# Moving the sign of a converted weight chunk behind the next exponentials on ScalarE

## The chip, the cores and the metric

The kernel runs on one core of one Trainium2 chip. The metric is device time in microseconds (us) from start to end of one execution; lower is better. The engines named below are TensorE (PE in the profile: matmuls and transposes), VectorE (DVE), ScalarE (ACT), GpSimd (POOL) and SyncE (SP, which here only issues DMAs). Each engine works through its own instruction stream in order; semaphores hold an instruction back until what it needs is done on another engine. DMAs move data between DRAM and on-chip memory.

## The reference

An attention block is followed by a Fourier mixing block, all in float32. There are 8 batches, 8 heads, 576 positions and 64 dimensions per head.

```python
scores = scale * np.matmul(q, k.transpose(0, 1, 3, 2))
thresh = np.max(scores, axis=-1, keepdims=True) - tau
scores = np.where(scores >= thresh, scores, -1000000000.0)
scores = scores - np.max(scores, axis=-1, keepdims=True)
attn = np.exp(scores)
attn = attn / (np.sum(attn, axis=-1, keepdims=True) + 1e-09)
x = np.matmul(attn, v)            # then (B,H,S,D) -> (B, S, H*D)
X = np.fft.fft(np.fft.fft(x, axis=1), axis=2)
u = x + np.real(X)
un = (u - mean(u)) / np.sqrt(var(u) + 1e-06)
out = u + np.maximum(un @ w_ch1, 0.0) @ w_ch2
```

The two weight matrices, w_ch1 (512 x 2048) and w_ch2 (2048 x 512), come in as float64, since the set-up casts q, k and v to float32 but not these. [...]the kernel converts them itself, from the raw bits.

## The kernel before

**Attention in steps.** Heads are taken in pairs, four pairs to a batch. A pair is worked off in five steps of 128 queries: steps t = 0 to 3 have both heads, step t = 4 takes the last 64 queries of both heads in one tile. A step's number is i, and 20 steps make a batch. `scores(i)` puts the scores into two PSUM tiles on TensorE (L430, L436). `softmax(i)` then runs, per head: the negated row maximum on VectorE (L453, `neg`), the exponential on ScalarE (L461, `e`), the threshold on ScalarE (L465, `thr`, once for both heads), and on VectorE the masking with its row sum (L469, which needs `thr` and `e`). After it come the reciprocal of the sums (L481) and, in the first batches, a broadcast copy of it on GpSimd (L493, `rec`). `transposed_weights(i - 1)` turns the masked weights of the step before with TensorE transposes (L530, L533, L548), and ScalarE copies them out of PSUM (`ends`, L536 and L540; `e_t`, L550 and L552). `weighted_values` multiplies them with V on TensorE (L577) and takes the result over on VectorE (L585). In t = 3, `prep_pair` transposes the next pair's K and Q on VectorE (L401 to L404), once their loads have come.

**Conversion of the weights.** It is spread over the first two batches, 16 chunks of 128 x 512 for w_ch1 in the first (one per step, steps 0 to 15) and 16 for w_ch2 in the second (the table `PLAN` gives the step of each; in three steps there are two chunks). `convert` is a generator, and each `yield` ends a stage:

- a DMA brings the raw 64-bit words into a stage in memory (L287); four stages in the tile `hs` are used in turn, in the second batch also other tiles;
- VectorE masks the mantissa bits (L297) and the exponent bits (L300) out of the high words;
- ScalarE scales the mantissa (L305), makes the bits of a power of two from the exponent (L308, `power`), and takes the sign of the high word, into the high word's own place (L311, `sign`);
- VectorE adds the low words (L313);
- GpSimd multiplies by the power (L318) and by the sign (L319), both in place in the weight tile.

In the first batch, `step(i)` issues the VectorE stage of chunk i before the transposed weights, and its ScalarE stage behind them. So on ScalarE the order around a step boundary is: `ends`, `e_t`, L305, L308, L311 of chunk i, and then the exponentials of step i + 1. The two stages left run inside `softmax(i + 1)`, as `meanwhile`, that is between the maxima and the exponentials: L313 on VectorE and L318 with L319 on GpSimd. The load of chunk i + 3 is issued at the end of step i. The second batch does the same through `advance(first)` and `advance(first - 1)`, where `first` counts the steps of that batch; when two chunks share a step, `advance` takes one stage of each in turn. There the steps also hold parts of other work: the Fourier mixing and the first matmuls of the channel part (`hidden`, L810, with its ReLU taken alternately by ScalarE, L815, and VectorE, L817), and the rows of finished tokens with their means and variances (`Rows.load`, L770 to L779; `Rows.factors`, L784).

**What sets the order.** For the first two batches the order of every engine is that of the program text (a manual schedule); from the third batch on only TensorE's order is written out by hand. In the first batch TensorE also runs a few matmuls on constants (`busy`, L112) that fill its time.

Of the kernel before, what the change touches and what calls it, by code (L numbers as in the profile page):

```python
# [47 lines left out]
def kernel(  # L48
# [12 lines left out]
    nc = tc.nc  # L61
# [218 lines left out]
    def convert(src, dst, raw, power):  # L280

        if src.dtype == FP32:
            nc.sync.dma_start(out=dst, in_=src)
            return
        nc.sync.dma_start(out=raw, in_=src.bitcast(INT32).rearrange("p (c n) -> p c n", c=2))  # L287
        pairs = raw.rearrange("p c (n two) -> p c n two", two=2)
        low, high = pairs[:, :, :, 0], pairs[:, :, :, 1]
        dst = dst.rearrange("p (c n) -> p c n", c=2)  # L290
        bits = dst.bitcast(INT32)
        power = power.rearrange("p (c n) -> p c n", c=2)
        sign = high.bitcast(FP32)

        yield

        nc.vector.tensor_scalar(  # L297
            out=bits, in0=high, scalar1=0xFFFFF, scalar2=None, op0=ALU.bitwise_and
        )
        nc.vector.tensor_scalar(  # L300
            out=power, in0=high, scalar1=20, scalar2=0x7FF,
            op0=ALU.logical_shift_right, op1=ALU.bitwise_and,
        )
        yield
        nc.scalar.activation(out=dst, in_=bits, func=ACT.Copy, bias=1.0, scale=2.0**-20)  # L305


        nc.scalar.activation(  # L308
            out=power, in_=power, func=ACT.Relu, bias=shift[:, :], scale=float(1 << 23)
        )  # L310
        nc.scalar.activation(out=sign, in_=high, func=ACT.Sign)  # L311
        yield
        nc.vector.scalar_tensor_tensor(  # L313
            out=dst, in0=low.bitcast(UINT32), scalar=2.0**-52, in1=dst,
            op0=ALU.mult, op1=ALU.add,
        )
        yield
        nc.gpsimd.tensor_tensor(out=dst, in0=dst, in1=power.bitcast(FP32), op=ALU.mult)  # L318
        nc.gpsimd.tensor_tensor(out=dst, in0=dst, in1=sign, op=ALU.mult)  # L319

    def chunk(src, dst, raw, power):
# [117 lines left out]
                )  # L439
        steps[i] = (sc, nh)  # L440

    def softmax(i, between=None, meanwhile=None):

        t = i % NT
        sc, nh = steps[i]
        neg = sb.tile([128, 2], FP32, tag="neg", bufs=3, name="neg")
        thr = sb.tile([128, 2], FP32, tag="thr", bufs=3, name="thr")
        den = sb.tile([128, 2], FP32, tag="den", bufs=3, name="den")


        e = sb.tile([128, 2 * S], FP32, tag="e", name="e")
        for j in range(nh):
            nc.vector.tensor_reduce(  # L453
                out=neg[:, j : j + 1], in_=sc[j][:, :, 0:HALF], axis=AXIS_XY, op=ALU.max,
                negate=True,
            )
        if meanwhile is not None:
            meanwhile()
        for j in range(nh):
            ej = e[:, S * j : S * (j + 1)].rearrange("p (c n) -> p c n", c=2)  # L460
            nc.scalar.activation(  # L461
                out=ej, in_=sc[j][:, :, 0:HALF], func=ACT.Exp, bias=neg[:, j : j + 1], scale=1.0
            )
            if j == 0:
                nc.scalar.activation(  # L465
                    out=thr[:, 0:nh], in_=neg[:, 0:nh], func=ACT.Identity,
                    bias=thr_off[:, :], scale=-1.0,
                )
            nc.vector.scalar_tensor_tensor(  # L469
                out=ej, in0=sc[j][:, :, 0:HALF], scalar=thr[:, j : j + 1], in1=ej,  # L470
                op0=ALU.is_ge, op1=ALU.mult, accum_out=den[:, j : j + 1],
            )

            nc.vector.tensor_scalar(
                out=den[:, j : j + 1], in0=den[:, j : j + 1], scalar1=1e-9, scalar2=None,
                op0=ALU.add,
            )
            if between is not None:
                between()
                between = None  # L480
        nc.vector.reciprocal(den[:, 0:nh], den[:, 0:nh])  # L481
        rec = None
        if normalized(i // NT):
            nc.vector.tensor_scalar(
                out=e[:, 0:S], in0=e[:, 0:S], scalar1=den[:, 0:1], scalar2=None, op0=ALU.mult
            )
            if nh == 2:
                nc.scalar.activation(  # L488
                    out=e[:, S : 2 * S], in_=e[:, S : 2 * S], func=ACT.Copy, scale=den[:, 1:2]
                )  # L490
        else:
            rec = sb.tile([128, 2 * D], FP32, tag="rec", name="rec")
            nc.gpsimd.tensor_copy(  # L493
                rec[:, :].rearrange("p (j d) -> p j d", j=nh), _repeated(den[:, 0:nh], 2 * D // nh)
            )
        if t == 4:
            nc.scalar.copy(e[:, S : S + 64], e[:, 512:S])
        steps[i] = (e, rec)
# [674 lines left out]
    def step(i):  # L1173

        n, t = divmod(i, NT)
        scores(i)

        def last_stages():
            run = chunks.pop(i - 1, None)
            for _ in range(2 if run else 0):  # L1180
                next(run, None)

        if t == 1 and n > 0:
            softmax(i, lambda: weighted_values(n - 1, 1), last_stages)
            load_v(n + 1)
        elif t == 3:
            softmax(i, lambda: weighted_values(n, 0), last_stages)
        else:
            softmax(i, None, last_stages)
        if t == 1 and n > 0:  # L1190
            pass
        elif later and later[0][0] <= i:
            later.pop(0)[1](i)
        else:
            busy(2 if i < NCHUNK else 1)
        if t == 2:
            scale_q(n + 1)
        if t == 3:
            prep_pair(n + 1)
        if t == 1:  # L1200
            prep_ends(n)
        if i in chunks:
            next(chunks[i])
        if i > 0:
            transposed_weights(i - 1)
        if i in chunks:
            next(chunks[i])
        while after and after[0][0] <= i:
            after.pop(0)[1]()
        if i > 0 and i + 3 < NCHUNK:  # L1210
            chunks[i + 3] = w1_chunk(i + 3)
        if t == 2 and n > 0:
            folds.append(fold_rows(n - 1))
        if folds and next(folds[0], True):
            folds.pop(0)
# [56 lines left out]
    def advance(at):  # L1272
        for run in chunks.get(at, ()):
            next(run, None)
# [34 lines left out]
    def second_batch(i):  # L1309

        nonlocal budget
        n, t = divmod(i, NT)
        first = i - per_batch
        if first != 1:
            scores(i)
        if first == 0:

            transposed_weights(i - 1)
        softmax(i, None, lambda: (advance(first - 1), advance(first - 1)))
        chunks.pop(first - 1, None)  # L1320
        transfers(first)
        fold_more()
        if first == 0:
            weighted_values(n - 1, 1)
            scores(i + 1)
            column_means(LAST)
            copy_mean(LAST)
            folds.append(fold_rows(n - 1))
            while folds:
                fold_more()  # L1330
            load_v(n + 1)
            start_batch(0)
            mix(3)
            mix(3)
        elif first == 1:
            mix(3)
            transposed_weights(i - 1)
            mix(2)
            mirrored(LAST)
            for c, eng in ((1, nc.vector), (3, nc.vector), (0, nc.gpsimd), (2, nc.gpsimd)):  # L1340
                less_mean(eng, LAST, c)
            advance(first)
            advance(first)
        elif first == 2:
            mix(2)
            transposed_weights(i - 1)
            mix(2)
            weighted_values(n, 0)
            advance(first)
            advance(first)  # L1350
        else:
            fill()
            transposed_weights(i - 1)
            advance(first)
            advance(first)
            fill()
            if t == 3:
                prep_pair(n + 1)
            fill()
            if t == 2:  # L1360
                weighted_values(n, 0)
            if t == 0:
                weighted_values(n - 1, 1)
                folds.append(fold_rows(n - 1))
                load_v(n + 1)
        if t == 1:
            prep_ends(n)
        if t == 2:
            scale_q(n + 1)
        if first == 16:  # L1370
            fold_halves(1)
        if first < 3:
            budget += 3 * per_slot
# [95 lines left out]
```

## Time and profile before

| | value |
|---|---|
| time, median of 5 runs | 1635.12 us (1634.53 to 1636.62) |
| time of the profiled execution | 1635.14 us |
| its span, first to last instruction | 1633.2 us |
| TensorE busy | 1583.7 us (97%) |
| VectorE busy | 1171.9 us (72%) |
| ScalarE busy | 816.3 us (50%) |
| GpSimd busy | 659.4 us (40%) |
| mean granted TensorE clock | 0.995 |

An engine's busy time is an average over parts of the program with different limits. Engine names in the rows below are the profile's; PEld is TensorE's weight load, which overlaps its matmuls. A row of the groups gives line, engine, operation, tiles, shapes and count, then the busy time and the mean of one instruction, then the engine's idle time before them with the one that ended it. A row in order of time gives start, duration, engine, line and operation, and in brackets the idle time of that engine before it and who ended it. Neighbouring instructions of an engine overlap a little in the records, so what one costs in its queue is the distance from its start to the next one's start.

### The profile page before, as it was taken

To read this page: it belongs to the slowest core of one execution; us is meant where nothing else is said; L and a number is where in the kernel's file an instruction comes from. 1 tells how busy PE (TensorE), PEld (TensorE's weight loads), DVE (VectorE), ACT (ScalarE), POOL (GpSimd) and SP (SyncE) were. 2 spreads that over 40 slices of the span, in tenths; PEclk is the share of its full clock that TensorE was granted. 3 is DMA by queue.
4 is the path that set the end of the run, shared out by engine and by line. 5 is a ranking of instruction groups with operands and counts; after the bars stand their busy time and mean duration, and the time that the engine had idled before them with its cause. 6 is when DMAs were issued, how large, how long until landed. Compare 5 with 4: busy or idle time off the path is not lost.

```text
span 1633.2 us, 27899 instructions
## 1 busy us (share of the span) xinstructions
PE 1583.7 (97%) x10346; PEld 1247.0 (76%) x10346; DVE 1171.9 (72%) x2518; ACT 816.3 (50%) x1738; POOL 659.4 (40%) x875
## 2 busy tenths in 40 slices
PE   8998889999999999999999999999999999999998
PEld 4555555577887888878888778877878788889998
DVE  7887896667757687857676868786787869664445
ACT  5775675544555454545354546454646455523111
POOL 6784674042421553244342244224352344125332
PEclk9999999999999999999999999999999999999999
DMA  6423222101110101110011010111111110000000
GB/s 160 124 56 113 74 74 57 36 22 22 18 41 15 33 12 43 23 28 16 22 23 36 15 36 9 43 23 29 23 22 36 23 28 2 14 7 7 14 14 14
DMA packets 203085, 57.41 MB, mean 35 GB/s; under 512 B 193828, under 2 KB 193830, under 8 KB 202951
## 3 DMA queue, kind: packets, MB, share of 16 engines
q1 hardware_dynamic: 200438, 55.34, 14.5%
q8 instruction: 82, 1.34, 0.4%
q10 hardware_dynamic: 2512, 0.30, 0.1%
q14 instruction: 53, 0.43, 0.1%
HBM read 46.02 MB, written 9.44 MB: 34 GB/s over the span
## 4 chain that ended last, share of the span: by engine, by line
PE 76%; DVE 14%; ACT 5%; issue 2%; POOL 1%; DMA 1%; SPq 0%; DVEq 0%; POOLq 0%; ACTq 0%
PE ph L914 24%; PE po L1078 20%; PE pv L577 9%; PE sc L430 7%; PE pw L548 6%; PE po L836 3%; DVE e L469 3%; DVE neg L453 2%; ACT e L461 2%; PE sc L436 1%; PE ph L810 1%; PE py L680 1%; PE pa L697 1%; PE pn L770 1%; DVE hs L1039 1%
## 5 line engine op out<-in xcount | busy, mean ns | idle before, releaser
L453 DVE TENSOR_REDUCE neg<-sc 128x1 f32<-128x576 f32 x288 | 207.1, 747 | 163.1 <-PE sc L430 151.9
L461 ACT ACTIVATE e<-sc,neg 128x576 f32<-128x576 f32 x288 | 212.2, 737 | 216.0 <-DVE neg L453 215.7
L469 DVE SCALAR_TENSOR_TENSOR e<-sc,thr,e 128x576 f32<-128x576 f32 x288 | 229.4, 811 | 49.9 <-ACT thr L465 48.4
L1078 PE MATMUL po<-w,hs 128*128 128x256 f32 x1024 | 246.9, 384 | 0.0
L1078 PEld LDWEIGHTS po<-w,hs 128*128 128x128 f32 x1024 | 186.5, 190 | 34.1 <-issue 13.0
L914 PE MATMUL ph<-u_t,w 128*128 128x128 f32 x1536 | 187.0, 276 | 0.0
L430 PE MATMUL sc<-kT,qT 64*128 64x288 f32 x1024 | 173.0, 431 | 11.8 <-DVE e L469 10.6
L914 PEld LDWEIGHTS ph<-u_t,w 128*128 128x128 f32 x1536 | 179.0, 192 | 5.0 <-issue 3.7
L548 PE MATMUL pw<-ident,e 128*128 128x128 f32 x1152 | 170.1, 274 | 8.1 <-ACT y_o L685 2.3
L550 ACT COPY e_t<-pw 128x512 f32<-128x512 f32 x256 | 148.6, 593 | 48.9 <-PE pw L548 48.2
L923 DVE TENSOR_TENSOR hs<-ph,hs 128x512 f32<-128x512 f32 x160 | 106.8, 684 | 69.5 <-PE ph L914 53.8
L548 PEld LDWEIGHTS pw<-ident,e 128*128 128x128 f32 x1152 | 134.4, 141 | 27.6 <-issue 4.2
L430 PEld LDWEIGHTS sc<-kT,qT 64*128 64x128 f32 x1024 | 95.4, 186 | 76.5 <-issue 36.5
L914 PE MATMUL ph<-t_u,s_w 128*128 128x128 f32 x1024 | 126.4, 277 | 2.2 <-POOL t_u L888 1.8
L914 PEld LDWEIGHTS ph<-t_u,s_w 128*128 128x128 f32 x1024 | 119.5, 192 | 7.7 <-issue 4.9
L1078 PE MATMUL po<-hs,s_tile 128*128 128x256 f32 x512 | 121.5, 381 | 0.0
L792 DVE SCALAR_TENSOR_TENSOR u<-po,rstd,u 128x256 f32<-128x256 f32 (+1 forms) x164 | 75.2, 482 | 64.0 <-PE po L1078 62.9
L488 ACT ACTIVATE e<-e,den 128x576 f32<-128x576 f32 x96 | 74.5, 776 | 76.5 <-DVE den L481 76.0
L1078 PEld LDWEIGHTS po<-hs,s_tile 128*128 128x128 f32 x512 | 94.0, 190 | 13.7 <-issue 2.5
L931 ACT ACTIVATE hs<-hs 128x512 f32<-128x512 f32 x112 | 69.2, 629 | 62.0 <-DVE hs L923 62.0
L610 POOL TENSOR_TENSOR half<-x 128x287 f32<-128x287 f32 x48 | 40.2, 858 | 119.8 <-ACT x L583 61.1
L1074 POOL TENSOR_TENSOR hs<-hs,s_tile 128x512 f32<-128x512 f32 x32 | 42.1, 1316 | 109.5 <-PE po L1078 86.5
(194 smaller groups left out, 2898.5 us busy)
## 6 DMA issues: line engine op xcount, KB each, us to landing
hs<-in_moe_w_ch_dram SPq DMA_DIRECT2D x23, 512.0 KB, 4.7
q_in<-in_q_dram SPq DMA_DIRECT2D x128, 72.0 KB, 2.3
out_dram<-u SPq DMA_DIRECT2D x36, 256.0 KB, 2.2
k_in<-in_k_dram SPq DMA_DIRECT2D x124, 72.0 KB, 2.3
v_in<-in_v_dram SPq DMA_DIRECT2D x64, 128.0 KB, 2.4
w<-in_moe_w_ch_dram SPq DMA_DIRECT2D x6, 512.0 KB, 4.7
stage<-in_moe_w_ch_dram SPq DMA_DIRECT2D x3, 512.0 KB, 3.9
v_in<-in_v_dram SPq DMA_DIRECT2D x64, 16.0 KB, 2.2
```

The costliest lines, as they stand in the source:

```text
L430: nc.tensor.matmul(sc[j][:, c, 0:HALF], qT[hp, 128 * t : 128 * t + 128], kT[hp, k0 + HALF * c : k0 + HALF * (c + 1)], start=True, stop=True,)
L453: nc.vector.tensor_reduce(out=neg[:, j : j + 1], in_=sc[j][:, :, 0:HALF], axis=AXIS_XY, op=ALU.max, negate=True,)
L461: nc.scalar.activation(out=ej, in_=sc[j][:, :, 0:HALF], func=ACT.Exp, bias=neg[:, j : j + 1], scale=1.0)
L469: nc.vector.scalar_tensor_tensor(out=ej, in0=sc[j][:, :, 0:HALF], scalar=thr[:, j : j + 1], in1=ej, op0=ALU.is_ge, op1=ALU.mult, accum_out ...
L488: nc.scalar.activation(out=e[:, S : 2 * S], in_=e[:, S : 2 * S], func=ACT.Copy, scale=den[:, 1:2])
L548: nc.tensor.transpose(pw[:, c, :], e[:, c0 : c0 + 128], ident[:, :])
L550: nc.scalar.copy(e_t[:, 4 * j : 4 * j + 4, qs], pw[:, :, :])
L577: nc.tensor.matmul(pv[64 * j : 64 * j + 64, 0:m], vt[:, 2 * c + j, :], e_t[:, 4 * j + c, 0:m] if c < 4 else ends[:, 0, 0:m], start=(c == 0 ...
L792: nc.vector.scalar_tensor_tensor(out=u, in0=product, scalar=self.rstd[:, t : t + 1], in1=u, op0=ALU.mult, op1=ALU.add,)
L914: nc.tensor.matmul(banks[name][:, 128 * q : 128 * q + 128], left[c][:, 512 * part + 128 * q : 512 * part + 128 * q + 128], right[c], start ...
L923: nc.vector.tensor_tensor(out=to, in0=bank, in1=to if other is None else other, op=ALU.add)
L1078: nc.tensor.matmul(bank[:, 0 : DM // 2], left[p], right[p], start=start and p == 0, stop=p == NK - 1, skip_group_check=True,)
```

## The change

The sign leaves the ScalarE stage of the conversion and becomes part of a new last stage, with GpSimd's product with it. `softmax` gets a further hook, `behind`, which it calls after the exponentials, thresholds and masking of all heads of the step and before the reciprocal. So the sign of chunk i follows the exponentials of step i + 1 on ScalarE, and stands ahead of the copies `ends` and `e_t` of that step. L313 and L318 stay where they were. In steps with two chunks the order of the GpSimd products becomes L318, L318, L319, L319 instead of L318, L319, L318, L319.

```diff
         nc.scalar.activation(
             out=power, in_=power, func=ACT.Relu, bias=shift[:, :], scale=float(1 << 23)
         )
-        nc.scalar.activation(out=sign, in_=high, func=ACT.Sign)
         yield
         nc.vector.scalar_tensor_tensor(
             out=dst, in0=low.bitcast(UINT32), scalar=2.0**-52, in1=dst,
...
         yield
         nc.gpsimd.tensor_tensor(out=dst, in0=dst, in1=power.bitcast(FP32), op=ALU.mult)
+        yield
+        nc.scalar.activation(out=sign, in_=high, func=ACT.Sign)
         nc.gpsimd.tensor_tensor(out=dst, in0=dst, in1=sign, op=ALU.mult)
...
-    def softmax(i, between=None, meanwhile=None):
+    def softmax(i, between=None, meanwhile=None, behind=None):
...
             if between is not None:
                 between()
                 between = None
+        if behind is not None:
+            behind()
         nc.vector.reciprocal(den[:, 0:nh], den[:, 0:nh])
...
-        def last_stages():
-            run = chunks.pop(i - 1, None)
-            for _ in range(2 if run else 0):
-                next(run, None)
+        def stages(count):
+            for _ in range(count if i - 1 in chunks else 0):
+                next(chunks[i - 1], None)
+
+        def next_stages():
+            stages(2)
+
+        def last_stage():
+            stages(1)
+            chunks.pop(i - 1, None)
 
         if t == 1 and n > 0:
-            softmax(i, lambda: weighted_values(n - 1, 1), last_stages)
+            softmax(i, lambda: weighted_values(n - 1, 1), next_stages, last_stage)
...
-        softmax(i, None, lambda: (advance(first - 1), advance(first - 1)))
+        softmax(
+            i, None, lambda: (advance(first - 1), advance(first - 1)), lambda: advance(first - 1)
+        )
```

The other two calls of `softmax` in `step` change in the same way.

More of the change, by code (lines that the diff above doesn't have):

```diff
@@ L1176, in step @@
         scores(i)
-        def last_stages():
-            run = chunks.pop(i - 1, None)
-            for _ in range(2 if run else 0):
-                next(run, None)
+        def stages(count):
[6 more added lines that the diff above has]
+            chunks.pop(i - 1, None)
         if t == 1 and n > 0:
-            softmax(i, lambda: weighted_values(n - 1, 1), last_stages)
+            softmax(i, lambda: weighted_values(n - 1, 1), next_stages, last_stage)
             load_v(n + 1)
         elif t == 3:
-            softmax(i, lambda: weighted_values(n, 0), last_stages)
+            softmax(i, lambda: weighted_values(n, 0), next_stages, last_stage)
         else:
-            softmax(i, None, last_stages)
+            softmax(i, None, next_stages, last_stage)
         if t == 1 and n > 0:
```

## The prediction

> **What bounds the kernel now.** The profiled execution took 1635.14 us; its span is 1633.2 us and 1.94 us lie around it. The median of the five runs is 1635.12 us, so sums made on the profile stand for the runs too. I read the busy time by stretch first (columns after the length: TensorE matmul, weight load, VectorE, ScalarE, GpSimd, each with its instruction count, then granted clock, DMA share, GB/s):
>
> ```profile
> 0.00:215.00 215.00, 190.52 (x953) 111.62 (x954) 180.55 (x403) 137.57 (x285) 144.12 (x213) 0.97 0.40 104
> 215.00:400.00 185.00, 180.80 (x978) 112.07 (x976) 129.03 (x288) 96.37 (x206) 65.81 (x92) 0.99 0.19 42
> 400.00:1633.00 1233.00, 1212.35 (x8419) 1023.31 (x8417) 862.34 (x1828) 582.32 (x1250) 449.50 (x571) 1.00 0.10 22
> ```
>
> From 400 us on TensorE is 98% busy. All 32 signs (L311) start between 16.5 and 253.5 us, and from 257 us the chain of waits runs on TensorE almost alone, so the change acts on some 240 us, and what it wins or loses there arrives at the end one for one: nothing behind 257 us gets new work. In those 240 us no engine is full (VectorE 84%, ScalarE 64%), so the bound is a loop between engines. The groups and the waits of VectorE up to 258 us (total, times, longest) show what a sign costs and who waits:
>
> ```profile
> L311 ACT ACTIVATE hs<-hs 128x512 f32<-128x512 int32 x23 | 15.3, 667 | 0.0
> ```
> ```profile
> DVE e L469 <- ACT thr L465: 15.8, 26, 1.5
> DVE stats L778 <- ACT u L776: 2.9, 1, 2.9
> ```
>
> A sign is 667 ns long, but the next instruction on ScalarE starts 0.56 us after it starts (36.40 to 36.96 below): that is its price in the queue. VectorE's masking (L469) waits for ScalarE's exponential and threshold, 15.8 us in 26 waits; one sign per chunk stands ahead of those. One step in order of time, all engines together:
>
> ```profile
> 34.83 0.39 DVE L297 TENSOR_SCALAR w<-hs 128x512 int32<-128x512 int32 x1
> 36.40 0.67 ACT L311 ACTIVATE hs<-hs 128x512 f32<-128x512 int32 x1
> 36.96 0.73 ACT L461 ACTIVATE e<-sc,neg 128x576 f32<-128x576 f32 x1
> 36.96 1.26 POOL L318 TENSOR_TENSOR w<-w,hs 128x512 f32<-128x512 f32 x1 [3.42 <-DVE w L313]
> 37.91 0.82 DVE L469 SCALAR_TENSOR_TENSOR e<-sc,thr,e 128x576 f32<-128x576 f32 x1 [1.09 <-ACT thr L465]
> 38.30 1.28 POOL L319 TENSOR_TENSOR w<-w,hs 128x512 f32<-128x512 f32 x1
> 39.04 0.83 DVE L297 TENSOR_SCALAR w<-hs 128x512 int32<-128x512 int32 x1
> 39.79 0.51 DVE L300 TENSOR_SCALAR hs<-hs 128x512 int32<-128x512 int32 x1
> 40.22 1.41 DVE L453 TENSOR_REDUCE neg<-sc 128x1 f32<-128x576 f32 x2
> ```
>
> Two things are to be seen. The masking waits 1.09 us, 0.56 of it for the sign. And L297, 0.39 us when GpSimd is idle, takes 0.83 us when it starts inside the product L319 and ends 0.29 us after it (38.30 + 1.28 = 39.58; 39.87). The same at 69.57 us, where L297 lasts 1.54 us under L319.
>
> **The change part by part.** *Removed ahead of the exponentials:* 32 x 0.56 us of ScalarE queue. It counts only where the exponential followed the sign without idle time and the masking then waited. In the first batch these waits are 0.29, 0.23, 0.33, 1.09, 0.57, 0.41, 0.46, 0.25, 0.32, 0.65, 0.40, 0.84 and 0.72 us; each cut to at most 0.56 gives 5.5 us. In three further steps the exponential waited for the maximum (0.56, 0.45, 0.63 us idle): nothing there. In the second batch 0.22, 0.68, 0.68, 0.68 and 0.54 us give 2.4 us. Once two signs stand ahead of the copies of a row tile:
>
> ```profile
> 183.84 0.65 ACT L311 ACTIVATE w<-w 128x512 f32<-128x512 int32 x1
> 184.39 0.25 ACT L775 COPY u<-pn 128x129 f32<-128x129 f32 x1
> 185.17 0.69 DVE L778 BATCH_NORM_STATS2 stats<-u 128x6 f32<-128x512 f32 x1 [2.91 <-ACT u L776]
> ```
>
> VectorE sits 2.91 us idle; two signs less bring it on 1.1 us earlier. Together 9.0 us at most.
>
> *What is late next.* Behind the masking stand L297 and L300 of the next chunk, and GpSimd's two products start from L313, which runs ahead of the masking and does not move. Here **a rule speaks against the change**: the Trainium skill, "SBUF — State Buffer", section "Who interferes with whom", says that a VectorE tensor_scalar in its two-port mode and a GpSimd instruction exclude each other for a whole instruction. The waits read alone promise 9.0 us. By the rule, and by the rows above, L297 that comes 0.56 us earlier only waits longer: in the step shown it would start at 38.48, still inside L319, and end at 39.87 as before; gain 0. From the rows, L319 ends 2.8 us after L313's end (0.15 + 1.34 + 1.29), while without any wait of the masking L297 is reached 2.05 us after it: in a plain two-head step it is always caught, its end is fixed at 3.08 us, and the wait removed is given back there. I go with the rule. What escapes it: steps in which K and Q transposes (1.8 us) come between masking and L297 (0.33 and 0.25 us); one where L297 started 0.3 us after L319's end (0.4 us); and the step shown, through TensorE: its next scores wait for the masking at 38.79 and TensorE then works through to 57 us, where the maximum waits 0.55 us for it (0.55 us). First batch: 1.5 us. Second batch: 0.2 at 164 us, 1.1 at 184 us, 0.5 at 234.8 us, where a sign stands ahead of the copy L815 that TensorE waits for (0.84 us): 1.8 us.
>
> *Added behind the exponentials:* the same 32 x 0.56 us. Queued behind are the copies of the transposed weights (ends, e_t), in the second batch L815 and L775 too. In most steps ScalarE idles there (0.5 to 1.8 us before ends, then again for L297), which hides it; without that cover a step costs 0.56 us, less what the exponential came earlier, so about 0.1 us. It is bare where the exponential does not come earlier or two signs follow: at 220 us
>
> ```profile
> 221.83 0.47 ACT L815 ACTIVATE hs<-ph 128x384 f32<-128x384 f32 x1
> 223.39 2.38 PE L577 MATMUL pv<-e_t,v_rev 128*64 128x320 f32 x16 [0.61 <-ACT e_t L552]
> ```
>
> two signs come in for one net 0.56 us, and TensorE, then the maximum at 227.5, lose 0.6 us; at 243 us the square root L784 follows, for which VectorE idles 0.99 us: minus 0.4. Losses: 1.0 us.
>
> *The product's new wait.* L319 now needs the sign. From the first exponential's start to the sign's end are 0.62 + 0.18 + 0.62 + 0.67 = 2.1 us; L318 ends 2.7 us after the first maximum, and the exponential starts at most 0.6 us after it. So the sign is done as L318 ends: 0 taken; the bounds are -0.1 and +0.3 us a step in the three steps with a copy of means (L1239). Behind the product are the reciprocals' copy (rec), which has nearly a step of room, and SyncE's next load into the stage, due three steps later in the first batch: 0. With two chunks the products now run L318, L318, L319, L319, the same four durations: 0. Once x_first's copy (0.39 us) passes ahead of L319: below 0.1 us.
>
> *Sum:* 1.5 + 1.8 - 1.0 = 2.3 us, so 1635.14 - 2.3 = **1632.8 us**. A measurement can tell about 0.2% here, 3.3 us, so this counts as no change.
>
> *TensorE's clock* adds a size I can't fix:
>
> ```profile
> 36.00:40.00 4.00, 2.52 (x15) 1.00 0.84 135
> 40.00:44.00 4.00, 4.00 (x10) 0.57 0.86 275
> ```
>
> TensorE idled 1.48 us before 38.79, and then ran some 3.4 us at half clock; four such dips (40, 71, 108, 213 us) cost up to 1.7 us each. The Trainium skill, "TensorE: Matmul & The Clock Gate", section "Why this matters for your kernels", warns of idle gaps of over about 3 us only. By the rule a gap shorter by 0.56 us changes nothing and a new gap of 1 us harms nothing; by the rows a dip can go or come. The rows decide: 0 taken, plus or minus 1.7 us for the range.
>
> **Rivals.** (a) *The lock does not hold the loop*: VectorE slips in between L318 and L319, or a dip goes. For it: L297 at 26.55 took 0.41 us in just that gap. Against it: both VectorE instructions must pass. It gives between 3.3 and 9.0 us; half of 9.0 and one dip of 1.7 make 6: 1629 us. (b) *Slower: the copies become the bound.* In 12 steps ScalarE goes from the exponential into ends, L815 or L775 without idle time (24.98, 86.44, 106.27, 179.00, 189.12, 196.66, 203.95, 221.83, 229.80, 236.11, 243.47, 255.45). If TensorE's accumulators there come free a sign later each time, that is 12 x 0.6 = 7 us, less the 2 us that still arrive: 1640 us. It decides from the sixth such step on. For it: TensorE already waits for these copies at 86.85, 223.39 and 256.66. Against it: it does so for 2 us in all. (c) *Nothing at all*: gains and losses cancel, 1635 us. That the change does not do what it says is out: in the changed program's order 32 signs stand behind exponentials and no other engine's order but GpSimd's, in the four places named, differs.
>
> **Chances.** Forecast 0.45, with its own range 1631.9 to 1634.5; (c) 0.12; (a) 0.30; (b) 0.13. Faster by over 0.2% is (a); within 0.2% the forecast and (c); slower (b). The range takes in most of (a) and the near half of (b): 1628.5 to 1637.0.
>
> **What would show it.** Right: the masking's wait for ScalarE falls from 15.8 to below 9 us, while the mean of L297 and L300 rises; L775's wait falls from 2.9 to 1.8 us; TensorE's wait for e_t at 223 us grows to 1.2 us; L319 never waits for a sign. The span to the last sign's step shortens by 2 us and the rest keeps its length. Wrong: L297 and L300 keep their durations and the gain is 5 us or more; or ends and e_t appear as releasers of TensorE in many steps.

## The result, and the profile after

| | before | after |
|---|---|---|
| time, median | 1635.18 us (47 runs, 1633.75 to 1637.50) | 1632.14 us (27 runs, 1630.13 to 1633.80) |
| profiled execution | 1635.14 us | 1632.78 us |
| its span | 1633.2 us | 1630.8 us |

The ratio of the times is 0.9979, with a 95% interval of 0.9974 to 0.9985: the change saves 3.0 us, 0.2%. The forecast was 1632.8 us. The stretches of the profile after (length; TensorE, weight load, VectorE, ScalarE, GpSimd with instruction counts; granted clock, DMA share, GB/s):

```profile
0.00:215.00 215.00, 189.62 (x959) 111.68 (x960) 185.74 (x405) 139.66 (x287) 147.16 (x215) 0.98 0.41 105
215.00:400.00 185.00, 180.61 (x990) 113.11 (x989) 127.69 (x290) 96.78 (x209) 64.30 (x90) 1.00 0.18 40
400.00:1630.00 1230.00, 1210.10 (x8400) 1021.87 (x8399) 860.02 (x1825) 580.44 (x1243) 448.83 (x571) 1.00 0.10 22
```

VectorE is now busy for 185.7 us of the first 215, where it was 180.6. The stretch reaches nearly 3 us further into the program than before, which accounts for only a part of these 5.2 us. Its waits up to 258 us (total, times, longest) show what was taken away:

```profile
DVE e L471 <- ACT thr L467: 7.9, 12, 1.5
DVE neg L455 <- PE sc L431: 6.6, 9, 1.3
...
DVE stats L782 <- ACT u L780: 1.8, 1, 1.8
DVE rstd L791 <- ACT rstd L788: 1.6, 1, 1.6
```

The masking waits 7.9 us in 12 waits, where it was 15.8 us in 26. So some 8 us of this wait went, and 3 us came out at the end. The rest is to be looked for in what stands behind the masking. A plain two-head step in the forecast's sense, 41.9 to 45.5 us in the trace after, shows it. Before:

```profile
42.80 0.82 DVE L469 SCALAR_TENSOR_TENSOR e<-sc,thr,e 128x576 f32<-128x576 f32 x1 [0.57 <-ACT thr L465]
...
43.72 1.30 POOL L319 TENSOR_TENSOR w<-w,hs 128x512 f32<-128x512 f32 x1
...
44.85 0.45 DVE L297 TENSOR_SCALAR w<-hs 128x512 int32<-128x512 int32 x1
...
45.22 0.51 DVE L300 TENSOR_SCALAR hs<-hs 128x512 int32<-128x512 int32 x1
```

After, with all engines in order of time (L320 is the product with the sign, L319 the sign):

```profile
41.95 0.80 DVE L471 SCALAR_TENSOR_TENSOR e<-sc,thr,e 128x576 f32<-128x576 f32 x1
42.17 1.28 POOL L317 TENSOR_TENSOR w<-w,hs 128x512 f32<-128x512 f32 x1 [2.35 <-DVE w L312]
42.28 0.66 ACT L319 ACTIVATE hs<-hs 128x512 f32<-128x512 int32 x1
...
43.53 1.29 POOL L320 TENSOR_TENSOR w<-w,hs 128x512 f32<-128x512 f32 x1
...
43.99 1.12 DVE L297 TENSOR_SCALAR w<-hs 128x512 int32<-128x512 int32 x1
...
45.02 0.51 DVE L300 TENSOR_SCALAR hs<-hs 128x512 int32<-128x512 int32 x1
```

Three things are to be seen. The masking's 0.57 us in brackets is gone. L297 comes 0.86 us earlier (44.85 to 43.99; 0.20 of that is older gain), starts inside the product L320 and lasts 1.12 us instead of 0.45; both times it ends about 0.3 us behind the product (44.85 + 0.45 = 45.30 and 43.72 + 1.30 = 45.02; 45.11 and 44.82). So the next maximum, which started at 45.65 us, starts at 45.45 us: just the 0.20 us that it was ahead one step earlier. The step gained nothing. And the product does not wait for the sign: it starts at 43.53 as L317 ends, when the sign has been done since 42.94.

Over all steps the same shows in the groups of VectorE up to 258 us (busy us, mean ns). Before:

```profile
L300 DVE TENSOR_SCALAR hs<-hs 128x512 int32<-128x512 int32 x23 | 19.1, 830 | 0.0
L297 DVE TENSOR_SCALAR w<-hs 128x512 int32<-128x512 int32 x23 | 18.0, 783 | 0.0
```

After:

```profile
L300 DVE TENSOR_SCALAR hs<-hs 128x512 int32<-128x512 int32 x23 | 20.0, 871 | 0.0
L297 DVE TENSOR_SCALAR w<-hs 128x512 int32<-128x512 int32 x23 | 19.6, 854 | 0.2 <-DMA hs<-in_moe_w_ch_dram 0.2
```

With the forms on other tiles, the 64 instructions of these two lines took 52.7 us before and 55.7 us after. So 3.0 us of the removed wait came back as longer instructions. Another part came back as other waits: VectorE's waits for TensorE's scores (`neg`) and for the weighted values (`x`, `pv`) went from 5.4 to 8.3 us, without the one that reaches across 258 us in both traces; 0.7 us of the difference stands at step 18, which the next table puts down to the clock.

To see where the time was won, I set the start of each step's first maximum (L453, now L455) in the one trace against the other. A number is the change of the distance against the step before. Steps are counted through both batches from 0, so the second batch begins at step 20. Step 0, which no moved sign can reach, came 0.15 us later and is left out of the sums; the other steps not named are within 0.1 us, and the sums take those in.

| where | measured, us | forecast, us |
|---|---|---|
| steps 4 and 9, K and Q transposes behind the masking | -0.42, -0.45 | -0.33, -0.25 |
| step 8, through TensorE | -0.38 | -0.55 |
| step 12, L297 clear of the product | -0.43 | -0.4 |
| steps 7, 10, 15 | -0.12, -0.12, -0.20 | 0 |
| steps 11 and 18, clock | +0.11, +0.87 | 0 |
| step 24, at 164 us | -0.51 | -0.2 |
| step 26, copies of a row tile | -1.16 | -1.1 |
| steps 27 and 30 | -0.10, -0.14 | 0 |
| step 31, two signs ahead of e_t | +0.59 | +0.6 |
| step 33, L815 earlier | -0.07 | -0.5 |
| step 34, sign ahead of the square root | +0.56 | +0.4 |

At 259 us the program is 1.76 us ahead. Without the rows of the clock the steps sum to -2.1 us in the first batch and -0.8 us in the second.

### The profile page after: what moved, and what is told of

Its sections match the earlier page's. It is cut to its first block, busy times and chain, and to the rows that moved or that the text cites. A ratio compares the mean times of both kernels' runs of the same rounds, so it can differ in the third digit from the quotient of the medians.

```text
span 1630.8 us, 27898 instructions
## 1 busy us (share of the span) xinstructions
PE 1580.3 (97%) x10346; PEld 1246.7 (76%) x10346; DVE 1173.5 (72%) x2518; ACT 816.9 (50%) x1738; POOL 660.3 (40%) x875
## 4 chain that ended last, share of the span: by engine, by line
PE 77%; DVE 14%; ACT 4%; POOL 2%; issue 2%; DMA 1%; SPq 1%; DVEq 0%; ACTq 0%; POOLq 0%
PE ph L918 24%; PE po L1082 20%; PE pv L581 9%; PE sc L431 7%; PE pw L552 6%; PE po L840 3%; DVE neg L455 2%; DVE e L471 2%; PE ph L814 2%; PE sc L437 1%; ACT e L463 1%; PE pn L774 1%; PE py L684 1%; PE pa L701 1%; DVE hs L1043 1%
## 5 line engine op out<-in xcount | busy, mean ns | idle before, releaser
L455 DVE TENSOR_REDUCE neg<-sc 128x1 f32<-128x576 f32 x288 | 207.2, 747 | 163.5 <-PE sc L431 151.8
L614 POOL TENSOR_TENSOR half<-x 128x287 f32<-128x287 f32 x48 | 40.5, 865 | 119.3 <-ACT x L587 61.0
```

What stands on the lines that cost most here:

```text
L455: nc.vector.tensor_reduce(out=neg[:, j : j + 1], in_=sc[j][:, :, 0:HALF], axis=AXIS_XY, op=ALU.max, negate=True,)
```

## The experiments

The theory at this point: each sign moved takes 0.56 us from ScalarE's queue, but GpSimd's two products lock out VectorE's L297 and L300, so that most of it is given back; what is left are the few steps in the table. The rivals: the copies behind the signs give it back; or the gain is a matter of the clock.

**One batch at a time.** A switch decides for each chunk whether its sign stands where it was or behind the exponentials. In e1_first_only it is moved in the first batch alone, in e2_second_only in the second alone.

```diff
-    def convert(src, dst, raw, power):
+    def convert(src, dst, raw, power, early):
...
+        if early:
+            nc.scalar.activation(out=sign, in_=high, func=ACT.Sign)
         yield
...
         nc.gpsimd.tensor_tensor(out=dst, in0=dst, in1=power.bitcast(FP32), op=ALU.mult)
-        yield
-        nc.scalar.activation(out=sign, in_=high, func=ACT.Sign)
+        if not early:
+            yield
+            nc.scalar.activation(out=sign, in_=high, func=ACT.Sign)
         nc.gpsimd.tensor_tensor(out=dst, in0=dst, in1=sign, op=ALU.mult)
```

> Only the 16 chunks of the first batch take their sign behind the exponentials; the second batch is as before. My sum: 1.5 us faster than before (ratio 0.9991); the profiles of before and after show the first batch 1.8 us shorter at its 17th step, 1.0 us once a dip of TensorE's clock has come later. The rival that all of the gain is in the first batch (masking waits there add up to 5.5 us): 3 us faster (0.998). The rival that it is all in the second batch: no change.

> Only the 16 chunks of the second batch take their sign behind the exponentials. My sum: +1.8 - 1.0 us, so 0.8 us faster than before (ratio 0.9995), of it 1.1 us at the one place where two signs stood ahead of the copies of a row tile. If the sum of both single moves falls short of the whole change (3.0 us), the two halves or the clock dips act together. Rival: all of the gain is here, 3 us (0.998).

Measured: the first batch alone 1632.57 us beside 1635.34 us, ratio 0.9982 (0.9973 to 0.9991); the second alone 1635.48 us, ratio 1.0003 (0.9994 to 1.0012). Nearly all that the change brings comes from the first batch. Step by step, e1_first_only repeats the gains at 4, 7, 8, 9, 10, 12 and 15 (-0.42, -0.12, -0.38, -0.48, -0.11, -0.33, -0.20; sum -2.0 us). E2_second_only repeats 26, 31, 33 and 34 (-1.15, +0.59, -0.07, +0.57). Two numbers stand in both runs and have nothing to do with a sign: -0.85 and -0.84 us at step 11, though the first batch of e2_second_only is the same as before, and +1.18 us at step 24 in each, though the second batch of e1_first_only is the same too. Both go with the clock, to which I come below: neither run has the dip that the trace before has at 71 us, and both have one at 162 to 167 us. That dip also hides the gain at step 24 in e2_second_only; e7_mixed_and_fill (below), which has no dip there, repeats it with -0.51 us. The interval of the second batch holds the -0.8 us of the steps as well as nothing; it does not tell them apart.

**Without the products.** Both GpSimd products of the conversion are taken out, from the kernel before (e3_before_no_products) and from the changed one (e4_after_no_products). The weights are then left without exponent and sign; all else is done. This shows what the move is worth when neither product can hold VectorE behind the masking.

```diff
-        nc.gpsimd.tensor_tensor(out=dst, in0=dst, in1=power.bitcast(FP32), op=ALU.mult)
...
-        nc.gpsimd.tensor_tensor(out=dst, in0=dst, in1=sign, op=ALU.mult)
```

> The kernel before without GpSimd's two products per chunk (power and sign); the weights are left without exponent and sign, all else is done. It is the partner of the next run. If the products hold VectorE's bit masks by the lock and with them the loop, this is faster than before by several us: L297 and L300 stay near 0.4 to 0.5 us each, where they now add up to about 48 us over 64 instructions against 29; some of that is hidden, so 5 to 15 us faster. If the products are harmless, within 2 us.

> The changed kernel without the same two products. My theory (the masking's wait that the change removes is given back because the products' end, not the masking, sets when the bit masks run): without the products the move of the signs is worth more against its partner run than the 3 us it is worth with them, 5 to 8 us of the 9.0 us of waits. Rival (the lock has no part, the gain was small because TensorE or the copies behind the exponentials take it back): the same 2 to 3 us as with the products, or less.

Measured: 1628.62 us (ratio 0.9959, 0.9947 to 0.9972) and 1619.45 us (0.9905, 0.9891 to 0.9918), both beside 1635.34 us. The same move that brings 3.0 us with the products brings 1628.62 - 1619.45 = 9.2 us without them. The groups of VectorE up to 258 us in e3_before_no_products, and then in e4_after_no_products:

```profile
L300 DVE TENSOR_SCALAR hs<-hs 128x512 int32<-128x512 int32 x23 | 12.9, 559 | 0.0
L297 DVE TENSOR_SCALAR w<-hs 128x512 int32<-128x512 int32 x23 | 11.6, 504 | 0.0
```

```profile
L300 DVE TENSOR_SCALAR hs<-hs 128x512 int32<-128x512 int32 x23 | 12.8, 555 | 0.0
L297 DVE TENSOR_SCALAR w<-hs 128x512 int32<-128x512 int32 x23 | 11.7, 511 | 0.7 <-DMA hs<-in_moe_w_ch_dram 0.7
```

With the products the mean of L297 rises with the move, from 783 to 854 ns; without them it hardly does, from 504 to 511 ns. The step of 42 us in e4_after_no_products, VectorE alone:

```profile
40.61 0.82 DVE L469 SCALAR_TENSOR_TENSOR e<-sc,thr,e 128x576 f32<-128x576 f32 x1 [0.44 <-ACT thr L465]
...
42.67 0.41 DVE L297 TENSOR_SCALAR w<-hs 128x512 int32<-128x512 int32 x1
42.99 0.52 DVE L300 TENSOR_SCALAR hs<-hs 128x512 int32<-128x512 int32 x1
```

L297 is through in 0.41 us. From e3 to e4 the plain steps 5, 6, 12 and 15 each gain 0.57, 0.58, 0.57 and 0.53 us, the whole 0.56 us of a sign; with the products they gained 0, 0, 0.43 and 0.20 us. That is what the theory claims. The copies behind the signs are the same in both pairs, so they are not what took it. Not all of the 9.2 us is the move's, though. In the traces, 2.8 us at step 2 (1.0 us of it lost again at step 3), 1.7 us at step 11 and 1.2 us at step 31 stand behind dips of the clock that e3 has and e4 has not; without steps 11 and 31 the trace gains 4.9 us from step 4 on. And the products leave with all that they do: buffers come free earlier too. The slowest run of e4 (1620.32 us) is still 5.2 us ahead of the fastest of e3 (1625.52 us). So the move is worth more without the products; how much more, between some 5 and 9 us, these runs leave open.

**The named gain and the named losses alone.** E8_only_step_5 moves only the signs of the second batch's step 5 (step 25 here, ahead of the copies of a row tile). E9_only_9_12 moves only those of its steps 9 and 12, where the forecast saw losses. In the switch above these are the steps left out of `early`:

```diff
+    EARLY_FIRST, EARLY_SECOND = True, (0, 1, 2, 3, 4, 6, 7, 8, 9, 10, 11, 12, 13, 14, 15)
```

```diff
+    EARLY_FIRST, EARLY_SECOND = True, (0, 1, 2, 3, 4, 5, 6, 7, 8, 10, 11, 13, 14, 15)
```

> The kernel before, with only the two chunks of the second batch's step 5 taking their signs behind the exponentials. It measures one place by itself: my price is 1.1 us for the maximum of the step after, and 0 in all other steps unless a dip moves. VectorE's wait for the row copies falls from 2.9 to 1.8 us.

> Theory (my two losses): of the kernel before, only the signs of the second batch's steps 9 (two) and 12 (one) are moved behind the exponentials, so only the losses I named remain: at step 31 of the trace (220 to 227 us) the maximum starts about 0.6 us later than in the kernel before, at step 34 (243 us) another 0.55 us later, and every other step of the first 258 us stands still but for clock dips of TensorE, which fall elsewhere from run to run; the row copies' wait at the end of the first batch stays near 2.9 us. Sum: about 1.15 us slower, 1636.3 us beside 1635.2. Rival (a sign costs nothing wherever it stands): no step moves, the time is that of before. One look cannot settle 1.15 us of time; the starts of the steps can.

Measured in e8_only_step_5: -1.17 us at step 26, everything else in the second batch within 0.13 us. The waits of VectorE up to 258 us:

```profile
DVE e L476 <- ACT thr L472: 16.0, 26, 1.5
...
DVE stats L787 <- ACT u L785: 1.8, 1, 1.8
```

The masking's wait stands as before (it was 15.8), and the wait for the row copies fell from 2.9 to 1.8 us by this one step. Its dips of the clock fall elsewhere (one before 260 us, where the trace before has four), so its single time, 1632.87 us, is not used.

In e9_only_9_12 no step up to 30 moves by more than 0.3 us. Then step 31 comes 0.98 us later and step 34 another 0.58 us. At step 34 it is the sign and nothing else. At step 31 ScalarE's rows are

```profile
221.39 0.69 ACT L324 ACTIVATE stage<-stage 128x512 f32<-128x512 int32 x1
221.95 0.68 ACT L324 ACTIVATE hs<-hs 128x512 f32<-128x512 int32 x1
222.52 0.48 ACT L824 ACTIVATE hs<-ph 128x384 f32<-128x384 f32 x1
222.89 0.52 ACT L549 COPY ends<-pe 64x128 f32<-64x128 f32 x2
223.43 0.59 ACT L561 COPY e_t<-pw 128x512 f32<-128x512 f32 x1
```

The copy e_t starts at 223.43 us and is 0.57 us later against its step than before (222.75 us, with the step 0.11 us later). But TensorE reached its matmul only at 224.48 us, with no wait for the copy, since its clock stood at half from 214.0 to 220.8 us, twice as long as in the trace before. So the +0.98 us there is the clock's. This run confirms one loss; the other is seen in the changed kernel and in e2_second_only, in both at +0.59 us. The single time, 1635.03 us beside 1635.61 us, is no evidence against a loss: the trace is 1.67 us behind at 261 us, and a later dip at 515 to 518 us that the kernel before had is missing here.

**Keeping the gains, leaving the losses.** E5_mixed moves all signs but those of steps 9 and 12 of the second batch:

```diff
+    EARLY_FIRST, EARLY_SECOND = False, (9, 12)
```

> All chunks take their sign behind the exponentials but three: the two of the second batch's step 9 and the one of step 12 keep it ahead, as before. In the profile of the changed kernel the maximum lost 0.59 us at the step after the two signs (the copies e_t then come late for TensorE) and 0.56 us at the square root of step 13. If these two losses are what they seem, this is 1.1 us faster than the changed kernel: 4 us faster than before (ratio 0.9974). If the losses only come elsewhere then, as the changed kernel (0.998).

Measured: 1631.01 us beside 1634.97 us, ratio 0.9974 (0.9965 to 0.9983), the lowest of any version that computes all; the interval overlaps that of the change (0.9974 to 0.9985), so the runs do not separate the two. The trace does: the loss at step 34 is gone (0.00 us there). ScalarE goes from the exponential straight into the copies:

```profile
241.67 0.72 ACT L468 ACTIVATE e<-sc,neg 128x576 f32<-128x576 f32 x1
242.29 0.36 ACT L545 COPY ends<-pe 128x256 f32<-128x256 f32 x1
```

At step 31 TensorE no longer waits for e_t, but its clock stood at half from 211.6 to 218.5 us in this execution too and hid what that is worth.

**Filling TensorE's gaps.** TensorE sits idle before the scores of some steps. If a dip follows from such a gap, one more matmul on constants there should prevent it. E6_before_and_fill does that to the kernel before, e7_mixed_and_fill to e5_mixed, which also gets one in the second batch.

```diff
     def step(i):
         n, t = divmod(i, NT)
+        if t == 0 and i > 0:
+            busy(1)
         scores(i)
...
         first = i - per_batch
+        if first == 10:
+            busy(1)
```

> The kernel before, with the three extra matmuls of the first batch alone. If gaps make the dips, those at 40 and 70 us go: the maximum of step 8 comes up to 0.55 us earlier and that of step 11 0.8 us, 1 us faster in all (0.9992), and the moved signs' part of the gain through TensorE at 57 us is shown to be partly one of its clock. If the gaps have no part: same dips, up to 1 us slower.

> As the run before, with one extra matmul on constants (0.4 us at full clock for each of its two passes) ahead of the scores where TensorE has its longest gaps: steps 5, 10 and 15 of the first batch and step 10 of the second. If a gap of 1.1 to 1.9 us on TensorE is what brings its clock down for 3.4 us, the dips at about 70 and 212 us go and it is 1 to 2 us faster than the run before (0.9965). If the clock only falls after gaps of 3 us, the fillers change nothing or cost up to 1 us. A dip can also come up elsewhere.

Measured: 1636.95 us (ratio 1.0012, 1.0003 to 1.0021) and 1634.26 us (0.9991, 0.9982 to 1.0000), both beside 1634.97 us. The fillers cost 2 us on the kernel before and about 3 us on e5_mixed. The dips at 40 and 71 us are absent in e6, but they are absent in e2_second_only as well, which has no filler, and e6 has new ones at 102.6 and 116.2 us, which stand at the +1.38 us of step 15 and the +0.86 us of step 18. E7, too, has dips, at 106.9 and 212.8 us. That a filler prevents dips fell.

## Why the prediction was right, and where it was not

**The bound and the give-back hold.** "By the rule, and by the rows above, L297 that comes 0.56 us earlier only waits longer": so it does in the step shown, and the pair without products shows for the whole that the move is worth more there. The masks took back 3.0 us by their length. The signs of it that the forecast named came: the masking's wait at 7.9 us (below 9), L297 from 783 to 854 ns, the row copies' wait from 2.9 to 1.8 us, no wait of the product for the sign. TensorE's wait for e_t grew from 0.61 to 1.01 us, where I had 1.2. Up to the last sign's step the trace is 1.76 us shorter, where I had 2; the rest did not keep its length, but is another 0.6 us shorter, which no moved sign explains. The 3.0 us lie within the forecast's own range, at its fast end, and 0.2% is the very line that was to part it from rival (a), so the size alone does not tell the two apart. That the masks grew longer does.

**First batch: 1.5 us forecast, 2.1 us by the steps.** The four escapes I named gave 1.7 us against my 1.53. The two steps with K and Q transposes were worth 0.42 and 0.45 us, not 0.33 and 0.25: I had put them at what the masking had waited there. Three steps that I had put at 0 (7, 10, 15) gave 0.12, 0.12 and 0.20 us, and the rows show how. At step 7 L297 had started 0.07 us behind the product's end (50.52 and 50.45 us), so it had a little room. At step 10 L297 had stood under the product (1.54 us) and L300 behind it (0.51 us); now L297 gets in with the product's start (0.41 us) and only L300 stands under it (1.52 us). At step 15 L297 had started together with the product, and L319 lasted 1.56 us; now it comes earlier, and the product lasts 1.37 us. None of the three is the plain step that the forecast had priced. The route through TensorE came, but not from the masking at 38.79 us that I named: at step 5 and at step 6 the maximum did not move at all. It began two steps later, where the masking's 0.41 us of wait went: the masking moved from 49.40 to 48.70 us (0.20 us of it won before), the scores behind it from 56.22 to 55.52 us, and the maximum at 57 us then waited 0.16 us for TensorE instead of 0.55 us. The dip at 40 us, which the trace before has and the trace after has not, is not the reason: in e2_second_only and e6_before_and_fill it is missing too, no sign of the first batch is moved, and step 8 stands within 0.02 us. The mechanism was right, its starting point was not.

**Second batch: 1.8 - 1.0 us forecast, 0.8 us by the steps, but by two errors that cancel.** The step at 234.8 us failed: "0.5 at 234.8 us, where a sign stands ahead of the copy L815 that TensorE waits for". Before, in VectorE's and GpSimd's rows:

```profile
234.27 0.67 DVE L313 SCALAR_TENSOR_TENSOR w<-hs,w 128x512 f32<-128x512 uint32 x1
...
234.73 1.62 POOL L610 TENSOR_TENSOR half<-x 128x287 f32<-128x287 f32 x2 [1.99 <-DMA x<-swap]
...
235.62 0.82 DVE L469 SCALAR_TENSOR_TENSOR e<-sc,thr,e 128x576 f32<-128x576 f32 x1 [0.68 <-ACT thr L465]
```

After:

```profile
231.97 2.00 POOL L614 TENSOR_TENSOR half<-x 128x287 f32<-128x287 f32 x2 [1.48 <-DMA x<-swap]
232.02 1.28 DVE L312 SCALAR_TENSOR_TENSOR w<-hs,w 128x512 f32<-128x512 uint32 x1
...
233.23 0.80 DVE L471 SCALAR_TENSOR_TENSOR e<-sc,thr,e 128x576 f32<-128x576 f32 x1
...
235.27 0.80 DVE L297 TENSOR_SCALAR w<-stage 128x512 int32<-128x512 int32 x1
...
235.99 1.52 DVE L300 TENSOR_SCALAR u_t<-stage 128x512 int32<-128x512 int32 x1
...
237.60 0.54 PEld L431 LDWEIGHTS sc<-kT,qT 64*128 64x128 f32 x6 [0.39 <-DVE u_t L300]
```

TensorE's wait for the copy did fall, from 0.84 to 0.30 us, and the masking's 0.68 us is gone. But an addition of the Fourier part on GpSimd (L614), which a DMA releases, now starts 0.05 us before VectorE's L312 instead of 0.46 us behind it, and L312 takes 1.28 us instead of 0.67. The wait was turned into the length of the instruction ahead of it, and L297 and L300 then stand under the products as before; the next scores on TensorE, whose weight load is the last row, start as L300 ends. I had looked for the lock behind the masking only, and for what TensorE waits for there only. Against that miss of 0.4 us stands the step at 164 us, 0.51 us where I had 0.2, as one L297 there got in ahead of a product (1.51 us long before, 0.57 us after), and 0.24 us at steps 27 and 30. The losses were 0.59 and 0.56 us for the 0.6 and 0.4 of the sum; the square root's wait (1.0 to 1.6 us in the list of waits) takes a sign's whole 0.56 us, since nothing lies between.

**The rivals.** That the copies become the bound fell: what is queued behind a sign cost time at two of the twelve places that I listed (221.83 and 243.47 us, there through the square root), 1.15 us in all, and not from step to step. That the lock does not hold fell with the groups. That nothing comes of it is excluded by the interval. **The clock**, for which I took 0 and plus or minus 1.7 us, is the part that the two profiled executions cannot settle: the steps of the change sum to -2.9 us, and the medians of the runs are 3.0 us apart, while the single span of after is 2.4 us shorter. I cannot say that the agreement of the first two numbers is more than luck within a few tenths.

## What to carry to other kernels

Before you price a wait that you remove, look whether something else already fixes the end of what stands behind it; here a lock between two engines did, and a good part of the removed wait came back as longer instructions, which no list of waits shows, so compare the mean durations too. Set the two traces against each other step by step on one marker: it shows which few steps carry a gain, and also which steps move although nothing in them was changed.

## What the runs showed of the hardware

The dips of TensorE's clock lie on a grid. In the kernel before they start at 40.21, 70.93, 108.48 and 214.29 us: the distances are 9, 11 and 31 times 3.413 us. Cut along that grid, each dip of this trace is one whole interval at half clock, and ahead of it stands one in which TensorE was busy for 33 to 62% (columns as in the stretches above):

```profile
36.80:40.21 3.41, 1.93 (x9) 0.98 (x9) 2.25 (x7) 2.52 (x8) 2.98 (x3) 1.00 0.84 134
40.21:43.62 3.41, 3.41 (x6) 1.23 (x6) 2.84 (x6) 3.18 (x7) 1.24 (x1) 0.50 0.91 296
...
210.87:214.28 3.41, 1.12 (x6) 0.67 (x7) 3.34 (x9) 2.23 (x7) 1.63 (x2) 1.00 0.62 134
214.28:217.69 3.41, 3.41 (x9) 1.73 (x6) 3.41 (x4) 2.07 (x5) 3.33 (x3) 0.50 0.84 143
```

In e2_second_only, whose first batch has the same instructions, the grid lies elsewhere: its dips start at 163.86 and 215.06 us, 15 times 3.413 us apart.

```profile
37.57:40.98 3.41, 2.16 (x9) 1.19 (x10) 2.97 (x8) 2.52 (x8) 2.40 (x3) 1.00 0.85 132
40.98:44.39 3.41, 2.23 (x11) 1.17 (x9) 2.81 (x7) 3.37 (x8) 1.91 (x2) 1.00 0.80 287
...
160.45:163.86 3.41, 1.46 (x5) 0.58 (x5) 3.38 (x7) 3.10 (x6) 3.41 (x5) 1.00 0.00 0
163.86:167.27 3.41, 3.41 (x9) 2.10 (x10) 3.34 (x8) 0.85 (x3) 3.33 (x3) 0.50 0.00 0
```

There TensorE's idle time before 39 us falls into one interval again, which is 63% busy, and no dip follows. The five executions that I laid on a grid (before, after, e1, e2 and e6) have 14 dips in the first 260 us, all on their own grid, and each grid at another offset. In e5_mixed and e9_only_9_12 one dip lasts two intervals (211.6 to 218.5 and 214.0 to 220.8 us). The grid is what the Trainium skill says of the window in "TensorE: Matmul & The Clock Gate", section "Part 1: The HAM clock gate (the "warmup" mystery)": 3413 ns long and free-running, not set back when a kernel starts. The same page's rule in "Why this matters for your kernels", which names only idle gaps of over about 3 us, does not cover these rows: the longest single gaps ahead of the 14 dips are 1.1 to 2.1 us.

What brings a dip stays open. Of those 14 intervals 13 were at most 62% busy and one 68%, but in the same executions intervals at 49 to 59% had no dip behind them, and in e7_mixed_and_fill one at 42% had none:

```profile
205.93:209.34 3.41, 1.43 (x12) 1.01 (x9) 3.37 (x7) 2.10 (x5) 0.04 (x1) 1.00 0.62 169
209.34:212.75 3.41, 1.66 (x7) 0.80 (x9) 3.34 (x8) 2.93 (x8) 3.41 (x3) 1.00 0.82 133
```

So in these traces the place of a dip belongs to the execution and not to the code alone, which fits that the fillers did not keep dips away and that the 47 runs of the kernel before lie up to 3.8 us apart. A step at which two traces differ by 0.7 to 1.4 us should be laid beside the clock first.
